# Rebalancing the first layer-norm tiles and moving two transposes in the head of an S5 + SwiGLU kernel

## The chip, the cores and the metric

One core of one Trainium2 chip. The metric is the device time of one execution in microseconds (us), smaller is better. The *span* that the profile shows is about 1.7 us shorter than that time, because it begins with the first profiled instruction and ends with the last. PE is TensorE, PEld its weight loads, DVE is VectorE, ACT is ScalarE, POOL is GpSimd, SP issues most DMAs. A time inside an execution is in us from the start of the span.

A run counts as slow when it is over 1.5% above the fastest of the same kernel.

## The reference, cut to what matters

The output is `x + A(xn) + B(xn)` with `xn = layernorm(x)` over 512 features, for 2048 rows. `A` is a linear state space (complex B matrix, scan over the rows, complex C matrix, skip term). `B` is a SwiGLU feed-forward of width 1376.

```python
xn = _layernorm(x)                                   # 2048 x 512
g, u = silu(xn @ w_gate), xn @ w_up                  # 512 x 1376 each
B = (g * u) @ w_down
Bu = einsum("bld,pd->blp", xn, B_bar)                # then h = Lam_bar*h + Bu[t], row by row
A = 2 * einsum("blp,dp->bld", hseq, Cmat).real + xn * Dskip
```

## The kernel before

The rows are worked in 4 chunks of 512 (4 tiles of 128 rows). Before PE can do anything useful, tile 0 must be loaded, normalised, transposed on PE and copied out of PSUM. To begin early, chunk 0's first seven gate column blocks are computed "in quarters": one 128-row tile after another, with the transposes of the next tile put between the matmuls. While waiting for tile 0, PE runs dummy matmuls.

The normalisation of the first tiles. Tile 0's left half is VectorE's, its right half ScalarE's; each tile has statistics (`b`, `s`), a reciprocal (`r`) and a normalisation in halves (`n`):

```python
def ln_half(a, h, order=()):
    cs = slice(h * 256, (h + 1) * 256)
    return g.add("dve", lambda e: e.tensor_scalar(out=xn_sb[:, a % NXN, cs], in0=x_sb[:, a, cs], scalar1=mv[:, a, 0:1], scalar2=rstd[:, a:a + 1],
                                                op0=ALU.subtract, op1=ALU.mult), ...)          # cut
# ... in ln_chunk0, VectorE's order:
for op, a, h in (("r", 0, 0), ("n", 0, 0), ("b", 1, 0), ("b", 1, 1), ("s", 1, 0), ("b", 2, 0),
                 ("r", 1, 0), ("n", 1, 0), ("n", 1, 1), ("b", 2, 1), ("s", 2, 0), ("b", 3, 0), ...):   # cut
    # ... with "r" of tile 0, ScalarE's part:
    g.add("act", lambda e: e.activation(out=xn_sb[:, 0, 256:512], in_=x_sb[:, 0, 256:512], func=AF.Identity, bias=nm0[:, 1:2], scale=rstd[:, 0:1]), ...)
```

The quarters. `place` says before which gate block (quarter, first contraction block, block number) the transposes of (tile, half) stand. All transposes of tiles 1 to 3 go through one PSUM bank, so each pair waits until the pair before has been copied out:

```python
place = {(0, 2, 4): (1, 0), (1, 0, 2): (1, 1), (1, 2, 2): (2, 0), (2, 0, 2): (2, 1), (2, 2, 1): (3, 0), (3, 0, 1): (3, 1)}
for q in range(4):
    for k0, k1 in (((0, 1), (1, 2), (2, 3), (3, 4)), ((0, 1), (1, 2), (2, 4)), ...)[q]:     # cut
        for n, (i, bk) in enumerate(tiles):                  # seven gate blocks
            if (q, k0, n) in place:
                xt_tile_fine(*place[(q, k0, n)])
            # ... k1 - k0 matmuls of 128 columns
```

After the quarters come one gate block of 512 columns, the up and gate blocks of chunk 0, and the state-space input `B_re`, `B_im`. Those two matrices come through DMA transposes. A DMA transpose is issued only when every DMA before it has landed, and every later DMA waits for it; so there is one long chain of DMAs: all first loads, B_re, B_im, the transpose of chunk 1, and so on.

```python
if xpose:
    after = after + tuple(dma_tasks)          # all DMAs before it
elif xp_state[0] is not None:
    after = after + (xp_state[0],)            # the last transpose
```

The order of instructions on VectorE, ScalarE and GpSimd is made by a list scheduler; that on PE and SP is the program's.

## Time and profile before

| | |
|---|---|
| time, median of 6 runs | 178.95 us (178.81 to 179.25) |
| PE busy | 173.5 us of the span of 177.2 us |
| first gate matmul of the quarters | 5.80 us |
| 512-column gate matmul after the quarters | 12.88 us |
| last addition on VectorE | starts 174.92 us |

The page of the kernel before: the span, the busy time and share of PE with its instructions, and two rows in which each digit is the busy share of a fortieth of the span, in tenths.

```profile
span 177.2 us, 2418 instructions
PE 173.5 (98%) x927; PEld 84.1 (47%) x935; DVE 162.7 (92%) x284; ACT 87.4 (49%) x116; POOL 11.1 (6%) x22
PE   8999999999999999999999999999999999999994
DMA  5892777662567500002000000001100000000032
```

PE is full from the first slice to the last. The DMA engines are loaded in the first 14 slices, and idle for most of the rest. So whatever a change does must show as an earlier or later start of PE's work, or as a gap in it.

PE's timeline in the head of the kernel before. The columns are start, duration of the merged group, engine, line, operation, tiles, shape, and count; matmuls overlap, so starts are the reliable part. Line L583 is the transposes, L478 the dummies, L804 the gate matmuls of the quarters, L760 the 512-column matmuls.

```profile
5.52 0.33 PE L583 MATMUL pb<-ident,xn_sb 128*128 128x128 bf16 x2
5.69 0.27 PE L478 MATMUL pb<-const-bfloat16-1.0 128*128 128x256 bf16 x1
5.80 1.17 PE L804 MATMUL pb<-xnT,wg 128*128 128x128 bf16 x18
6.80 0.28 PE L583 MATMUL pb<-ident,xn_sb 128*128 128x128 bf16 x2
...
8.63 0.28 PE L583 MATMUL pb<-ident,xn_sb 128*128 128x128 bf16 x2
8.74 0.83 PE L804 MATMUL pb<-xnT,wg 128*128 128x128 bf16 x12
9.53 0.27 PE L583 MATMUL pb<-ident,xn_sb 128*128 128x128 bf16 x2
...
12.88 0.38 PE L760 MATMUL pb<-xnT,wg 128*128 128x512 bf16 x1
```

ScalarE in the same stretch: its piece of tile 0 (L549), the first copy out of PSUM (an "eviction", L593), and the eviction of the pair of 8.63:

```profile
4.87 0.60 ACT L549 ACTIVATE xn_sb<-x_sb,nm,rstd 128x256 bf16<-128x256 bf16 x1
5.38 0.45 ACT L593 ACTIVATE xnT<-pb 128x128 bf16<-128x128 bf16 x2
8.95 0.45 ACT L593 ACTIVATE xnT<-pb 128x128 bf16<-128x128 bf16 x2 [0.62 <-PE pb L583]
```

Twelve matmuls at 55.8 ns are 0.67 us; from 8.74 to 9.53 it is 0.79. So 0.12 us is lost before the transposes at 9.53: they wait for ScalarE to copy the pair of 8.63 out of the shared bank, which takes it until 9.40.

The weight loads around the first use of B_im; in brackets, how long the loads stood idle, and what ended that:

```profile
23.89 0.74 PEld L881 LDWEIGHTS pb<-xnT,BT 128*128 128x128 bf16 x4
24.81 1.76 PEld L881 LDWEIGHTS pb<-xnT,BT 128*128 128x128 bf16 x9 [0.18 <-DMA BT<-in_A_B_im_dram]
```

```profile
174.92 0.29 DVE L983 TENSOR_TENSOR x_sb<-pb,x_sb 128x128 bf16<-128x128 f32 x1 [0.21 <-PE pb L978]
```

### The profile page before, as it was taken

To read this page: it belongs to the slowest core of one execution; us is meant where nothing else is said; L and a number is where in the kernel's file an instruction comes from. 1 tells how busy PE (TensorE), PEld (TensorE's weight loads), DVE (VectorE), ACT (ScalarE), POOL (GpSimd) and SP (SyncE) were. 2 spreads that over 40 slices of the span, in tenths; PEclk is the share of its full clock that TensorE was granted. 3 is DMA by queue.
4 is the path that set the end of the run, shared out by engine and by line. 5 is a ranking of instruction groups with operands and counts; after the bars stand their busy time and mean duration, and the time that the engine had idled before them with its cause. 6 is when DMAs were issued, how large, how long until landed. Compare 5 with 4: busy or idle time off the path is not lost.

```text
span 177.2 us, 2418 instructions
## 1 busy us (share of the span) xinstructions
PE 173.5 (98%) x927; PEld 84.1 (47%) x935; DVE 162.7 (92%) x284; ACT 87.4 (49%) x116; POOL 11.1 (6%) x22
## 2 busy tenths in 40 slices
PE   8999999999999999999999999999999999999994
PEld 2894444444444444444444444444444444444644
DVE  2965999899899999999999999999999999999943
ACT  4679989989979779220456554000365520000000
POOL 3040500050050000000000000000000000000000
DMA  5892777662567500002000000001100000000032
GB/s 167 273 372 81 122 129 112 171 143 70 142 130 269 113 7 0 0 4 89 31 0 0 0 0 4 0 0 59 59 0 4 0 0 0 0 0 32 31 110 68
DMA packets 22966, 12.37 MB, mean 70 GB/s; under 512 B 15180, under 2 KB 22956, under 8 KB 22956
## 3 DMA queue, kind: packets, MB, share of 16 engines
q1 hardware_dynamic: 22652, 11.77, 25.3%
q10 hardware_dynamic: 304, 0.46, 0.8%
q8 instruction: 7, 0.11, 0.3%
q14 instruction: 3, 0.02, 0.0%
HBM read 6.46 MB, written 2.10 MB: 48 GB/s over the span
## 4 chain that ended last, share of the span: by engine, by line
PE 60%; DMA 17%; DVE 15%; SPq 3%; issue 1%; POOL 1%; ACT 1%
PE pb L760 19%; PE pb L964 19%; PE pb L978 16%; DMA x_sb<-in_A_x_dram 7%; DVE rot L921 4%; PE pb L881 4%; SPq L405 3%; DVE st L483 3%; DMA xnT<-xn_sb 3%; DMA hss<-in_A_C_im_dram 3%; DVE rot L912 3%; DMA hss<-in_A_C_re_dram 2%; DMA dsk<-in_A_Dskip_dram 2%; PE pb L975 2%; DVE hT L832 2%
## 5 line engine op out<-in xcount | busy, mean ns | idle before, releaser
L921 DVE TENSOR_TENSOR_SCAN rot<-sm,car,rot 128x512 bf16<-128x512 f32 x32 | 38.9, 1266 | 0.0
L772 ACT ACTIVATE sg<-pb 128x1024 bf16<-128x1024 f32 x20 | 20.1, 1021 | 32.5 <-PE pb L760 31.8
L964 PE MATMUL pb<-wd,hT 128*128 128x512 bf16 (+2 forms) x176 | 34.5, 355 | 0.3 <-ACT uf L868 0.2
L978 PE MATMUL pb<-W,hss 128*128 128x512 bf16 (+2 forms) x140 | 29.7, 355 | 0.2
L760 PE MATMUL pb<-xnT,wu 128*128 128x512 bf16 x120 | 27.9, 379 | 0.0
L964 PEld LDWEIGHTS pb<-wd,hT 128*128 128x128 bf16 x180 | 16.8, 98 | 18.2 <-issue 0.4
L830 ACT ACTIVATE uf<-pb 128x1024 bf16<-128x1024 f32 x20 | 20.5, 1024 | 8.3 <-PE pb L760 8.0
L760 PE MATMUL pb<-xnT,wg 128*128 128x512 bf16 x92 | 21.8, 380 | 0.0
L881 PE MATMUL pb<-xnT,BT 128*128 128x512 bf16 x96 | 21.0, 380 | 0.0
L978 PEld LDWEIGHTS pb<-W,hss 128*128 128x128 bf16 x144 | 13.5, 97 | 14.4
L888 ACT ACTIVATE u_sb<-pb 128x1024 bf16<-128x1024 f32 x16 | 16.2, 1019 | 4.6 <-PE pb L881 4.6
L760 PEld LDWEIGHTS pb<-xnT,wu 128*128 128x128 bf16 x120 | 11.7, 98 | 14.2 <-issue 0.2
L881 PEld LDWEIGHTS pb<-xnT,BT 128*128 128x128 bf16 x96 | 9.4, 98 | 11.3 <-DMA BT<-in_A_B_im_dram 0.2
L983 DVE TENSOR_TENSOR x_sb<-pb,x_sb 128x512 bf16<-128x512 f32 (+2 forms) x18 | 11.1, 629 | 3.6 <-PE pb L978 3.0
L760 PEld LDWEIGHTS pb<-xnT,wg 128*128 128x128 bf16 x92 | 9.0, 98 | 10.6
L832 DVE TENSOR_TENSOR hT<-sg,uf 128x1024 bf16<-128x1024 bf16 x20 | 13.4, 681 | 0.3 <-ACT uf L830 0.3
L912 DVE TENSOR_TENSOR rot<-u_sb,cosT 128x2048 bf16<-128x2048 bf16 x8 | 9.7, 1218 | 0.1
L912 DVE TENSOR_TENSOR rot<-rot,sin 128x2048 bf16<-128x2048 bf16 x8 | 9.8, 1220 | 0.0
L912 DVE TENSOR_TENSOR rot<-u_sb,sin 128x2048 bf16<-128x2048 bf16 x8 | 9.7, 1217 | 0.0
L912 DVE TENSOR_TENSOR rot<-rot,cosT 128x2048 bf16<-128x2048 bf16 x8 | 9.7, 1215 | 0.0
L483 DVE BATCH_NORM_STATS2 st<-x_sb 128x6 f32<-128x512 bf16 x12 | 7.4, 680 | 2.4 <-DMA x_sb<-in_A_x_dram 2.4
L912 DVE TENSOR_TENSOR rot<-rot 128x2048 bf16<-128x2048 bf16 x8 | 9.6, 1217 | 0.0
(93 smaller groups left out, 180.9 us busy)
## 6 DMA issues: line engine op xcount, KB each, us to landing
out_dram<-x_sb SPq DMA_DIRECT2D x15, 128.0 KB, 1.7
x_sb<-in_A_x_dram SPq DMA_DIRECT2D x3, 512.0 KB, 4.7
wd<-in_B_w_down_dram SPq DMA_DIRECT2D x1, 1280.0 KB, 7.2
wu<-in_B_w_up_dram SPq DMA_DIRECT2D x1, 768.0 KB, 4.8
wu<-in_B_w_up_dram SPq DMA_DIRECT2D x1, 608.0 KB, 6.9
x_sb<-in_A_x_dram SPq DMA_DIRECT2D x4, 128.0 KB, 3.1
wg<-in_B_w_gate_dram SPq DMA_DIRECT2D x1, 480.0 KB, 5.8
wg<-in_B_w_gate_dram ACTq DMA_DIRECT2D x1, 448.0 KB, 3.8
```

The lines of the kernel that those rows point to most:

```text
L483: return g.add("dve", lambda e, a=a: e.bn_stats(out=st[:, a % 8, :], in_=x_sb[:, a, :]), reads=[("x", a)], writes=[("st", a % 8), ("st0", ...
L760: inst = e.matmul(pbank[0:fs, bk, :].rearrange("p (j t) -> p j t", j=4), lhsT=w[:, kt, i * 128:i * 128 + fs], rhs=xnT[c][:, :, kt, :], sta ...
L772: g.add("act", lambda e: e.activation(out=sg[rows, sl, 0:n, :].rearrange("p a t -> p (a t)"), in_=pair_f32(rows, bk, 512 * n), func=AF.Sil ...
L830: g.add("act", lambda e: e.activation(out=uf[rows, ul, 0:n, :].rearrange("p a t -> p (a t)"), in_=pair_f32(rows, bk, 512 * n), func=AF.Ide ...
L832: g.add("dve", lambda e: e.tensor_tensor(out=hT[rows, hb, i0:i0 + n, :], in0=sg[rows, sl, 0:n, :], in1=uf[rows, ul, 0:n, :], op=ALU.mult), ...
L881: inst = e.matmul(pbank[:, bk, :].rearrange("p (j t) -> p j t", j=4), lhsT=BT[:, ri, kt, pt * 128:(pt + 1) * 128], rhs=xnT[c][:, :, kt, :] ...
L888: g.add("act", lambda e: e.activation(out=u_sb[:, us].rearrange("p r t -> p (r t)"), in_=pair_f32(slice(0, 128), b0), func=AF.Identity), r ...
L912: tt = lambda out, a, b, op, r, w, nm: g.add("dve", lambda e: e.tensor_tensor(out=out, in0=a, in1=b, op=op), reads=r, writes=w, name="%s_% ...
L921: g.add("dve", lambda e, A0=A0, A1=A1, k=k, ri=ri, pt=pt: e.tensor_tensor_scan(out=A1[:, k, ri, :], data0=rr[:, pt:pt + 1].to_broadcast([1 ...
L964: inst = e.matmul(pbank[:, bk, 0:nc_], lhsT=hT[0:fs, hb, i, lt * 128:(lt + 1) * 128], rhs=wd[0:fs, i, c0:c0 + nc_], start=(i == 0), stop=F ...
L978: inst = e.matmul(pbank[:, bk, 0:nc_], lhsT=hss[:, hb, pt, ri, lt * 128:(lt + 1) * 128], rhs=W12[:, ri, pt, c0:c0 + nc_], start=False, sto ...
L983: g.add("dve", lambda e, bk=bk, a=a, c0=c0, nc_=nc_: e.tensor_tensor(out=x_sb[:, a, c0:c0 + nc_], in0=pbank[:, bk, 0:nc_], in1=x_sb[:, a, ...
```

## The change

The intent is a shorter head: give ScalarE less of tile 0, since PE waits for its half; take tile 1's statistics in one operation instead of two and a longer merge; and transpose the first halves of tiles 1 and 2 one gate block sooner, so that they are copied out before PE needs the bank and the data.

```diff
         def ln_half(a, h, order=()):
-            cs = slice(h * 256, (h + 1) * 256)
+            cs = slice(0, 384) if a == 0 else slice(h * 256, (h + 1) * 256)
 ...
-  in_=st0[:, a].rearrange("p h s -> p (h s)")[:, 0:6 if a == 0 else 12]),
-  reads=[("st0", a, 0), ("st0", a, 1)], writes=[("mv", a)], ...
+  in_=st0[:, a].rearrange("p h s -> p (h s)")[:, 0:6 if a < 2 else 12]),
+  reads=[("st0", a, h) for h in range(1 if a < 2 else 2)], writes=[("mv", a)], ...
 ...
-            for op, a, h in (("r", 0, 0), ("n", 0, 0), ("b", 1, 0), ("b", 1, 1), ("s", 1, 0), ("b", 2, 0),
+            for op, a, h in (("r", 0, 0), ("n", 0, 0), ("B", 1, 0), ("s", 1, 0), ("b", 2, 0),
 ...
-  e.activation(out=xn_sb[:, 0, 256:512], in_=x_sb[:, 0, 256:512], ...
+  e.activation(out=xn_sb[:, 0, 384:512], in_=x_sb[:, 0, 384:512], ...
 ...
-            place = {(0, 2, 4): (1, 0), (1, 0, 2): (1, 1), (1, 2, 2): (2, 0), ...
+            place = {(0, 2, 3): (1, 0), (1, 0, 2): (1, 1), (1, 2, 1): (2, 0), ...
```

Cut: the second transposes of a tile now wait for both of its parts, and "B" calls the 512-column statistics. After the head, the order of instructions is the same on every engine.

More of the change, by code (lines that the diff above doesn't have):

```diff
@@ L522, in ln_stat0 @@
         def ln_stat0(a, order):
-            t = g.add("dve", lambda e: e.bn_aggr(out=mv[:, a, :], in_=st0[:, a].rearrange("p h s -> p (h s)")[:, 0:6 if a == 0 else 12]),
-                      reads=[("st0", a, 0), ("st0", a, 1)], writes=[("mv", a)], name="bnag%d" % a, est=160, order=order)
+            t = g.add("dve", lambda e: e.bn_aggr(out=mv[:, a, :], in_=st0[:, a].rearrange("p h s -> p (h s)")[:, 0:6 if a < 2 else 12]),
+                      reads=[("st0", a, h) for h in range(1 if a < 2 else 2)], writes=[("mv", a)], name="bnag%d" % a, est=160, order=order)
             hold["sd%d" % a] = g.add("act", lambda e: e.activation(out=sd0[:, a:a + 1], in_=mv[:, a, 1:2], func=AF.Sqrt, bias=epst[:, 0:1]),
@@ L548, in ln_chunk0 @@
                         hold["nmr0"] = g.tasks[-1]
-                        g.add("act", lambda e: e.activation(out=xn_sb[:, 0, 256:512], in_=x_sb[:, 0, 256:512], func=AF.Identity, bias=nm0[:, 1:2], scale=rstd[:, 0:1]),
-                              reads=[("x", 0), ("rstd", 0), ("nm0", 1)], writes=[("xh", 0, 1)], name="xn0_1", est=430)
+                        g.add("act", lambda e: e.activation(out=xn_sb[:, 0, 384:512], in_=x_sb[:, 0, 384:512], func=AF.Identity, bias=nm0[:, 1:2], scale=rstd[:, 0:1]),
+                              reads=[("x", 0), ("rstd", 0), ("nm0", 1)], writes=[("xh", 0, 1)], name="xn0_1", est=400)
                         hold["xa01"] = g.tasks[-1]
@@ L555, in ln_chunk0 @@
                     last = bn_half(a, h, (last,))
+                elif op == "B":
+                    last = bn_full(a, (last,))
                 elif op == "p":
@@ L585, in tr2 @@
                 return inst
-            g.add("pe", tr2, reads=[("xh", a, h), ("ident",)], writes=BK(slot), name="xT%d_%d" % (a, h), est=2 * 64, ninst=2)
+            g.add("pe", tr2, reads=[("xh", a, k) for k in range(h + 1)] + [("ident",)], writes=BK(slot), name="xT%d_%d" % (a, h), est=2 * 64, ninst=2)
             dst, src = xnT[0][:, a % 4, 2 * h:2 * h + 2, :], ptr[:, slot, 0:256].rearrange("p (k t) -> p k t", k=2)
@@ L794, in ffn_gate_quarters @@
             pe_warm(1, 256, tiles[-2][1])
-            place = {(0, 2, 4): (1, 0), (1, 0, 2): (1, 1), (1, 2, 2): (2, 0), (2, 0, 2): (2, 1), (2, 2, 1): (3, 0), (3, 0, 1): (3, 1)}
+            place = {(0, 2, 3): (1, 0), (1, 0, 2): (1, 1), (1, 2, 1): (2, 0), (2, 0, 2): (2, 1), (2, 2, 1): (3, 0), (3, 0, 1): (3, 1)}
             for q in range(4):
```

## The prediction

> **What bounds the kernel now.** TensorE: the page has PE busy 98% of the 177.2 us span, and the table by stretches has it busy for all of 5.80 to 12.88 us (chunk 0's gate matmuls, in quarters) and 12.88 to 24.10. The change touches only the head, before 12.9 us. What counts is when the first gate matmul starts (5.80), stalls inside the quarters, and whether an earlier head reaches the end.
>
> **The edits, costed.**
> - VectorE takes 384 columns of tile 0, not 256: the timeline has 345 ns for 256 and 406 ns for 512, so +30 ns. The first transposes (4.97 us) and ScalarE's first eviction (5.38) start up to 0.03 later.
> - ScalarE takes 128 columns, not 256 (measured 600 ns). The Trainium skill, "ScalarE: Activation LUTs", What ACT_TABLE_LOAD costs, has 0.833 ns per element and 93 ns per pointer operand over 186 ns: 585 ns for 256 with two pointers, in agreement. So -107 ns, an estimate. The waits view has PE waiting 0.3 us for this result; the second transposes should move from 5.52 to about 5.42.
> - The first gate matmul also needs the first eviction, which gets no earlier: gain 0.03 to 0.1 us (start about 5.73).
> - Tile 1 statistics: two half ops take 0.75 us, one full op 0.695, the aggregate of 6 values 183 ns instead of 208: -0.08, less the +0.03 above. Tile 1's normalisation comes 0.05 earlier, enough for its earlier transposes, with at most 0.05 of wait.
> - Transposes one gate tile sooner: two 56 ns matmuls move behind them, no work changes. At 55.8 ns a matmul and 0.11 us a pair of transposes, the quarters have some 0.15 us of stall in 7.08, 0.12 of it before 9.53 us, where PE waits for tile 2's eviction. That should go.
>
> Head gain: about 0.15 us (0.05 to 0.25); quarters end near 12.73.
>
> **How much reaches the end: almost nothing.** At 24.81 us PE waits for the DMA transpose of B_im. The waits view says 0.18 us; at the pitch of 0.216 us the load was due at 24.75, so the loss is 0.06. The chain of waits has only DMAs there: x tiles 4 to 7 land at 15.99, B_re runs from 16.03 to 20.48, B_im from 20.50 to 24.8. These wait for no engine, the DMA share is 0.98 from 5.8 to 12.9 us, and the edit moves no DMA. PE arrives earlier and waits longer by as much. A second such place is 67.71 us, where PE waits 0.16 us for a ScalarE eviction behind DMA and VectorE work. The order of instructions after the head is unchanged on every engine.
>
> **Predicted: 178.8 us** (before 178.9), 8 in 10 between 178.4 and 179.2. Faster by over 2%: 0.005; within 2%: 0.99; slower: 0.005.
>
> **What would show it.** Right: second transposes near 5.42, first gate matmul 5.70 to 5.80, transposes of tile 1 near 6.68 and of tile 2 near 8.45 without a wait, the gap before 9.5 gone, quarters ending near 12.73; then PE's weight load waiting about 0.3 us for B_im, still at 24.8, and PE's times as before from there. Wrong: B_im landing earlier with the head, or PE's times after 24.8 shifted by the head gain; or a later head (transposes waiting for normalisation, gate matmul after 5.85), which would reach the end nearly in full, since only 0.06 us of slack is there.
>
> **What could make it wrong.** DMA landings that scatter by more than the head gain, and the scatter of runs (178.81 to 179.25), larger than the edit's effect.

## More of the kernel before

PE where the last transpose is first used (the second line), and VectorE's last addition:

```profile
63.82 1.03 PE L843 MATMUL pb<-scrC,wg 128*128 128x512 bf16 x4
64.68 1.03 PE L843 MATMUL pb<-xnT,wg 128*128 128x512 bf16 x4
```

## The result, and the profile after

| | before | after |
|---|---|---|
| median of 6 runs, us | 178.95 (178.81 to 179.25) | 178.98 (178.77 to 179.23) |
| ratio of fast runs | | 1.0001 (0.9988 to 1.0014) |
| first gate matmul, us | 5.80 | 5.52 |
| tile 1's transposes, us | 6.80 | 6.75 |
| 512-column gate matmul, us | 12.88 | 12.72 |
| last addition starts, us | 174.92 | 175.10 |

Ratios are the mean time of one kernel's fast runs over that of the other's of the same rounds, so they are not quite the ratios of the medians. The time is the same; the interval is about 0.2 us to either side. The head ends 0.16 us earlier, and in this profile the end comes 0.18 us later.

The page of the changed kernel:

```profile
span 177.4 us, 2425 instructions
PE 173.9 (98%) x935; PEld 83.8 (47%) x935; DVE 162.5 (92%) x283; ACT 86.9 (49%) x116; POOL 11.1 (6%) x22
```

The counts of PE differ only because 8 matmul records are missing in the trace before. Line numbers behind the edits are 2 higher. PE's timeline in the head of the changed kernel, and ScalarE's piece of tile 0 and first eviction:

```profile
5.29 0.29 PE L585 MATMUL pb<-ident,xn_sb 128*128 128x128 bf16 x2
5.41 0.27 PE L478 MATMUL pb<-const-bfloat16-1.0 128*128 128x256 bf16 x1
5.52 1.39 PE L806 MATMUL pb<-xnT,wg 128*128 128x128 bf16 x17
6.75 0.27 PE L585 MATMUL pb<-ident,xn_sb 128*128 128x128 bf16 x2
...
8.48 0.28 PE L585 MATMUL pb<-ident,xn_sb 128*128 128x128 bf16 x2
8.59 0.94 PE L806 MATMUL pb<-xnT,wg 128*128 128x128 bf16 x14
9.37 0.28 PE L585 MATMUL pb<-ident,xn_sb 128*128 128x128 bf16 x2
...
12.72 0.59 PE L762 MATMUL pb<-xnT,wg 128*128 128x512 bf16 x2
```

```profile
4.74 0.49 ACT L549 ACTIVATE xn_sb<-x_sb,nm,rstd 128x128 bf16<-128x128 bf16 x1
5.17 0.45 ACT L595 ACTIVATE xnT<-pb 128x128 bf16<-128x128 bf16 x2
```

Two things are to be seen. From 8.59 to 9.37 there are now 14 matmuls in 0.78 us, at 55.8 ns each: the stall is gone. But 17 matmuls from 5.52 to 6.75 take 1.23 us where 0.95 would do. The starts of the single matmuls have a gap of 0.28 us before 6.58 us: the third contraction block's gate weights landed at 6.45 us here, at 6.07 in the trace before. So the early start (5.52) was lost again at 6.58, which is also when the same matmul ran before (5.80 + 14 x 0.0558 = 6.58). Only the stalls taken out of the quarters remain.

The weight loads at B_im, PE at the last transpose, and the last addition, after:

```profile
23.73 0.74 PEld L883 LDWEIGHTS pb<-xnT,BT 128*128 128x128 bf16 x4
24.75 1.67 PEld L883 LDWEIGHTS pb<-xnT,BT 128*128 128x128 bf16 x9 [0.27 <-DMA BT<-in_A_B_im_dram]
```

```profile
63.66 1.03 PE L845 MATMUL pb<-scrC,wg 128*128 128x512 bf16 x4
64.85 1.04 PE L845 MATMUL pb<-xnT,wg 128*128 128x512 bf16 x4 [0.17 <-DMA xnT<-xn_sb]
```

```profile
175.10 0.29 DVE L985 TENSOR_TENSOR x_sb<-pb,x_sb 128x128 bf16<-128x128 f32 x1 [0.21 <-PE pb L980]
```

The loads waited 0.27 us for B_im, but the matmuls show no gap over 0.03 us at 24.8: loads run ahead of matmuls. PE was still 0.16 us ahead of the trace before at 37.76 (37.92 before) and at 63.66 (63.82 before). Then four matmuls that were due at 64.52 (4 x 0.2157 after 63.66) came at 64.85: the last transpose had landed only at 64.81 us (62.74 in the trace before). That gap of 0.33 us turned a lead of 0.16 into a lag of 0.18. Its cause lies earlier in the DMA chain: the transpose is issued when the loads of `w_down` have landed, which was at 60.48 us here and at 58.43 before. The change touches no DMA, so I took it for scatter and tested that.

### The profile page after: what moved, and what is told of

It is laid out like the page before. It is cut to its first block, busy times and chain, and to the rows that moved or that the text cites. A ratio compares the mean times of both kernels' runs of the same rounds, so it can differ in the third digit from the quotient of the medians.

```text
span 177.4 us, 2425 instructions
## 1 busy us (share of the span) xinstructions
PE 173.9 (98%) x935; PEld 83.8 (47%) x935; DVE 162.5 (92%) x283; ACT 86.9 (49%) x116; POOL 11.1 (6%) x22
## 3 DMA queue, kind: packets, MB, share of 16 engines
HBM read 6.46 MB, written 2.10 MB: 48 GB/s over the span
## 4 chain that ended last, share of the span: by engine, by line
PE 62%; DMA 19%; DVE 7%; ACT 4%; SPq 3%; POOL 1%; issue 1%; ACTq 0%
PE pb L966 20%; PE pb L762 19%; PE pb L980 16%; DMA x_sb<-in_A_x_dram 7%; DMA xnT<-xn_sb 5%; PE pb L883 4%; SPq L405 3%; DVE st L483 3%; DMA hss<-in_A_C_im_dram 3%; DMA hss<-in_A_C_re_dram 2%; DMA dsk<-in_A_Dskip_dram 2%; PE pb L977 2%; ACT xn_sb L507 2%; DVE hT L834 1%; PE pb L855 1%
## 5 line engine op out<-in xcount | busy, mean ns | idle before, releaser
L966 PE MATMUL pb<-wd,hT 128*128 128x512 bf16 (+2 forms) x180 | 35.2, 355 | 0.0
L980 PE MATMUL pb<-W,hss 128*128 128x512 bf16 (+2 forms) x144 | 30.3, 355 | 0.0
```

Source lines behind the costliest of these rows:

```text
L966: inst = e.matmul(pbank[:, bk, 0:nc_], lhsT=hT[0:fs, hb, i, lt * 128:(lt + 1) * 128], rhs=wd[0:fs, i, c0:c0 + nc_], start=(i == 0), stop=F ...
L980: inst = e.matmul(pbank[:, bk, 0:nc_], lhsT=hss[:, hb, pt, ri, lt * 128:(lt + 1) * 128], rhs=W12[:, ri, pt, c0:c0 + nc_], start=False, sto ...
```

## The experiments

My theories going in: (A) the prediction's, that the DMA chain swallows any head gain at 24.8 us; (B) that the gain reaches the end unless the run happens to be late somewhere; and, for the head, which of the three parts does the work. The kernels that change PE's amount or order of work keep the order of all other engines on purpose: the estimates that the scheduler sees were left as they were, and the orders were compared.

### Before, again

No edit.

> The kernel before, unchanged, profiled a second time, to see what scatters by itself. If head and DMA times scatter from run to run: the first gate matmul between 5.5 and 5.8 us (depending on when TensorE's clock steps up), x tiles 4 to 7 landing anywhere from 15.9 to 16.4 us, B_im used first at 24.7 to 25.0, and the span 177.1 to 177.5. If instead these differences between the two traces are caused by the change: first gate matmul again at 5.80 within 0.03, landing at 15.99, and no wait for the last transpose (xnT of chunk 3) near 64.8.

Time 179.3 us against 178.82 for another run of the same kernel. The first gate matmul came at 5.99 us, outside the 5.5 to 5.8 that I expected, since its weights landed at 5.86 us (5.01 in the first trace), the 512-column gate matmul at 13.17 and the last addition at 175.21. So the same kernel moves by 0.29 us from one trace to the next, in the head and, undiminished, at the end. The x tiles 4 to 7 landed at 16.32 (15.97 in the first trace), the last transpose at 63.47 (62.74). The scatter is larger than the change.

### One part at a time

Only the transposes' place:

```diff
-            place = {(0, 2, 4): (1, 0), (1, 0, 2): (1, 1), (1, 2, 2): (2, 0), ...
+            place = {(0, 2, 3): (1, 0), (1, 0, 2): (1, 1), (1, 2, 1): (2, 0), ...
```

> Only the earlier place of the first-half transposes of tiles 1 and 2. My theory: the stall of 0.12 us before the transposes near 9.5 us goes, and the stretch from the first gate matmul to the 512-column gate matmul takes 6.95 to 7.0 us instead of 7.08, less whatever the gate weights' landing adds; a wait of at most 0.1 us may appear before tile 1's transposes, whose normalisation is not earlier here. Rival (the gain in the quarters comes from the statistics or the split): the stretch stays at 7.05 to 7.1.

The whole stretch took 7.42 us, against the 6.95 to 7.0 that I expected, but not by stalls. PE's timeline of this kernel:

```profile
5.52 0.42 PE L478 MATMUL pb<-const-bfloat16-1.0 128*128 128x256 bf16 x1
5.73 1.61 PE L804 MATMUL pb<-xnT,wg 128*128 128x128 bf16 x17
7.17 0.28 PE L583 MATMUL pb<-ident,xn_sb 128*128 128x128 bf16 x2
```

The starts of its first gate matmuls are 0.107 us apart up to 6.69 us, and 0.056 after. This is TensorE's clock at half rate: in this run it stepped up at about 6.7 us, in the changed kernel's profile before 4.85. The dummy of 256 columns just before the first gate matmul (0.42 us here, 0.27 after the step) tells at a glance which it is. From tile 1's transposes on, it was 5.98 us with no gap over 0.03 us, so the part does what was expected.

Only the 384/128 split of tile 0:

```diff
-            cs = slice(h * 256, (h + 1) * 256)
+            cs = slice(0, 384) if a == 0 else slice(h * 256, (h + 1) * 256)
-  in_=x_sb[:, 0, 256:512], func=AF.Identity, bias=nm0[:, 1:2] ...
+  in_=x_sb[:, 0, 384:512], func=AF.Identity, bias=nm0[:, 1:2] ...
```

> Only the 384/128 split of tile 0. My theory: the ScalarE piece takes about 0.49 us instead of 0.60, the second transposes come 0.07 to 0.12 us sooner after the reciprocal, the first gate matmul 0.03 to 0.1 us sooner after it; the stall of 0.12 us before 9.5 us stays. Rival (the whole 0.28 us of the first gate matmul came from the split): 0.25 us or more from the same reciprocal to the first gate matmul.

ScalarE's piece took 493 ns (600 before), and the second transposes came 1.13 us after the reciprocal's start (5.33 after 4.20), against 1.24 to 1.26 in the two traces of the kernel before: 0.11 to 0.13 us sooner. In all 14 traces it was 1.07 to 1.14 us in the eight with the split and 1.18 to 1.25 in the six without. The first gate matmul came at 5.73 us, 1.54 us after the reciprocal's start (1.52 in the first trace before), so the 0.03 to 0.1 us that I expected there did not show in this run; and, with the clock slow up to about 6.7 us, tile 1's transposes only at 7.22. Two stalls of 0.12 us stayed in the quarters. So the split gives its 0.1 us at the second transposes, and not the whole 0.28 of the first gate matmul, whose parts are listed further below.

Only tile 1's statistics in one operation:

```diff
-  ("n", 0, 0), ("b", 1, 0), ("b", 1, 1), ("s", 1, 0), ("b", 2, 0),
+  ("n", 0, 0), ("B", 1, 0), ("s", 1, 0), ("b", 2, 0),
-  [:, 0:6 if a == 0 else 12]
+  [:, 0:6 if a < 2 else 12]
```

> Only the one-op statistics of tile 1. My theory: tile 1's aggregate starts about 0.05 us sooner after tile 0's normalisation, its normalisation 0.05 to 0.08 sooner, and nothing on PE moves, since PE reached tile 1's transposes without waiting before; stretch from the first gate matmul to the 512-column one 7.05 to 7.1 us as before. Rival (tile 1's normalisation was holding PE): the transposes of tile 1 come 0.05 us or more sooner after the first gate matmul.

The aggregate began 0.98 us after tile 0's normalisation (5.37 after 4.39), where before it was 1.04 and 1.05: 0.06 sooner. Tile 1's normalisation, which I expected sooner too, was not: 1.84 us after tile 0's, against 1.81 in the first trace before. The quarters kept their stall (0.12 us before 9.55), and from tile 1's transposes to the 512-column matmul it was 6.08 us, as before. Nothing on PE moved. The stretch from the first gate matmul was 7.28 us and not the 7.05 to 7.1 expected: 0.20 of it is a gap at 6.34 us, with the third block's gate weights landing at 6.46. The time, 180.13 us, came from elsewhere. PE's timeline near 58 us:

```profile
59.78 3.63 PE L883 MATMUL pb<-scrC,BT 128*128 128x512 bf16 x16 [0.96 <-ACT sg L774]
```

PE stood still for 1.12 us between 58.44 and 59.78, waiting for a PSUM bank that ScalarE empties. ScalarE had itself idled 1.8 us for VectorE before normalising chunk 3. Smaller gaps at this place turn up in other runs below, with both orders of the head.

### Taking work out of the head

Half of the contraction is left out of four up blocks, 8 matmuls of 512 columns or 1.73 us of PE. Its output is wrong, which doesn't matter for the time.

```diff
-                ffn_mm(c, i0 + k, "u", bk + k)
+                ffn_mm(c, i0 + k, "u", bk + k, 2 if c == 0 and ip < 2 else KT)
```

> The changed kernel with 8 matmuls of 512 columns (4 x 2, the up projection of chunk 0, half the contraction left out) taken from PE between 13.6 and 24 us; wrong on purpose, all other engines' order kept. It makes the head gain 8 x 0.216 = 1.73 us instead of 0.15. My theory (the DMA chain fixes when PE may go on at 24.8 us): PE waits about 1.9 to 2.0 us for B_im instead of 0.27, later PE times unmoved, span and time unchanged within 0.15 us. Rival (the wait at 24.8 us is an accident of the profile, and a head gain reaches the end): time 1.5 to 1.8 us lower, near 177.3.

Ratio 0.9993 (0.9965 to 1.0021); median 178.98 us, before 179.16 on the same chip. The rival's 1.5 us is excluded. The weight loads, PE near 59 us and the last addition:

```profile
25.16 1.41 PEld L883 LDWEIGHTS pb<-xnT,BT 128*128 128x128 bf16 x8 [1.87 <-DMA BT<-in_A_B_im_dram]
```

```profile
59.26 3.63 PE L883 MATMUL pb<-scrC,BT 128*128 128x512 bf16 x16 [0.25 <-ACT sg L774]
```

```profile
175.55 0.29 DVE L985 TENSOR_TENSOR x_sb<-pb,x_sb 128x128 bf16<-128x128 f32 x1 [0.21 <-PE pb L980]
```

Here the matmuls did stop, for 1.55 us, at B_im, which landed at 25.11; another 0.42 us went at 59.26. Together they ate the 1.73 us, and 0.24 more. A large head gain is thus swallowed at 24.8 us, as theory A has it.

### Adding work to the head

Six dummy matmuls, 1.29 us, just behind the quarters, for both kernels:

```diff
+            pe_warm(6, 512, xt_pair[0])
+            g.tasks[-1].est = 0.0
             ffn_mm(0, NQ, "g", xt_pair[0])
```

> The changed kernel with 6 dummy matmuls of 512 columns (1.29 us) put on PE just after the quarters, order otherwise kept. My theory: about 0.2 us of it is swallowed by the wait for B_im, and up to 0.2 us more by the wait for the last transpose near 64.8 us, the rest reaches the end: time 0.85 to 1.15 us higher than before, near 179.95. Rival (the DMA chain alone sets the time up to 67 us): time within 0.3 us of before. Second rival (there is no slack at all): 1.3 us higher.

> The kernel before with the same 6 dummy matmuls (1.29 us) after the quarters as head_plus6 has. PE then comes 1.2 us later to B_im and to the last transpose, so neither should hold it, and a head difference should pass to the end undiminished. Revised theory: from tile 1's transposes to the 512-column gate matmul 7.38 to 7.47 us (head_plus6 has 7.35), the last addition 162.04 us after that matmul, no PE gap after it but the switch to 64 columns; time 179.9 to 180.5, its difference from head_plus6 (180.13) too small for the times. Rival (the gap goes to some later wait even so): a PE gap after 25 us, and the last addition more than 162.1 us after the gate matmul.

Changed kernel with the dummies: median 180.13 us, ratio to before 1.0058 (1.0033 to 1.0082), which is 0.6 to 1.5 us. Kernel before with the dummies: 180.48 us, 1.0081 (1.0065 to 1.0096). The first rival of head_plus6 (less than 0.3 us) is excluded; 0.85 to 1.15 and 1.29 are not told apart by the times. The traces do it. The last additions, first of the changed kernel, then of the kernel before:

```profile
176.06 0.29 DVE L987 TENSOR_TENSOR x_sb<-pb,x_sb 128x128 bf16<-128x128 f32 x1 [0.22 <-PE pb L982]
```

```profile
175.97 0.29 DVE L985 TENSOR_TENSOR x_sb<-pb,x_sb 128x128 bf16<-128x128 f32 x1 [0.21 <-PE pb L980]
```

The 512-column gate matmul ran at 14.03 and at 13.93 us. To the last addition it was 162.03 and 162.04 us, without a gap that other runs don't have. With PE late, nothing is given back anywhere: a microsecond in the head is a microsecond at the end. The kernel before was even 0.10 us ahead of the changed one here, because its head began earlier: the first gate matmul ran at 5.54 us against 5.73, after a reciprocal that was 0.09 us sooner and with the clock stepping up at about 3.7 us instead of 5.6. (In neither did PE wait for the third block's weights.) That one run of each cannot be turned into a difference of the kernels.

### Giving B_im and the last transpose more room

A helper moves one group of PE's matmuls behind another after scheduling. `after_slack` puts B_re of the second block ahead of B_im of the first; `two_gates` and `late_gates` also ask for the last transpose later, in two ways.

```diff
+        pe_after("mm_b0_0_1", "mm_b0_1_0")           # all three
+        pe_after("mm_ul0", "mm_g1_%d" % FL)          # two_gates
+        pe_after("mm_g3_%d" % FL, "mm_ul2")          # late_gates
```

> The changed kernel with two groups of 4 PE matmuls exchanged (B_re of the second block before B_im of the first), so that B_im is needed 0.86 us later. My theory: the wait of 0.2 to 0.3 us at 24.8 goes; PE runs 0.2 to 0.3 us earlier until the last transpose near 64.8 us, where it waits by so much longer if that lands late, as in the changed kernel's profile, and passes where it lands early, as in the profile before; time 0 to 0.25 us lower. Rival (B_im's wait doesn't matter): the same times, PE at 64 us as before.

> As after_slack, and the left-over up matmuls of chunks 0 and 1 moved ahead of the gate matmuls of chunks 2 and 3, so that the last transpose is needed 1.7 us later as well. My theory: neither wait is left, PE runs unbroken from the quarters to the end, the head gain arrives: time 0.2 to 0.45 us lower than before, near 178.6. Rival (something else, ScalarE's or VectorE's chain at 67 us, fixes the rest): within 0.1 us of before.

> The changed kernel with B_im and the last transpose both needed 0.86 us later (B_re of the second block before B_im of the first; the left-over gate matmuls of chunk 3 behind the left-over up matmuls, without a further switch between 64 and 128 columns). Theory: no PE gap at 24.8 or near 64.5, end 162.04 us after the 512-column gate matmul; time 0.1 to 0.3 us below before's (ratio 0.998 to 0.9995), which 5 rounds may or may not tell from 1. Rival (the late chain through VectorE and ScalarE near 56 us holds PE): a gap near 58 us and no gain.

Ratios to before: after_slack 0.9986 (0.9959 to 1.0013), two_gates 0.9994 (0.9969 to 1.0018), late_gates 0.9998 (0.9966 to 1.003). None is told from 1. The gaps at 24.8 and 64.5 us were absent in all three traces. two_gates paid 0.2 us for two more switches between matmuls that use 128 and those that use 64 columns of PE's array (`128*128` and `128*64` in the profile; 0.09 to 0.10 us each). late_gates met the third place instead, which my theory for it had not counted:

```profile
58.95 3.63 PE L883 MATMUL pb<-scrC,BT 128*128 128x512 bf16 x16 [0.28 <-ACT sg L774]
```

That is a gap of 0.45 us, behind the chain through VectorE and ScalarE, and its last addition started at 175.25. In this trace its rival was right. No version was found that beats both kernels by an amount the times can show.

### Changed kernel and place alone, with more times

No edit to the changed kernel; the place alone as above.

> The changed kernel, unchanged, for more times and a second trace. Revised theory: the transposes one tile sooner always take 0.12 to 0.2 us of stall out of the quarters, so from tile 1's transposes to the 512-column gate matmul 5.97 to 6.03 us (before 6.08 and 6.17); the wait for B_im takes no more than 0.05 us of it, and from the 512-column gate matmul to the last addition it is 162.04 us plus the later stalls of the run. So the head gain reaches the end wherever nothing else is late, on average 0.05 to 0.2 us, below what the times can show (ratio 0.998 to 1.0015). Rival (the prediction: swallowed at 24.8 us in every run): the first B_im matmul waits for its landing, the stretch from the 512-column gate matmul to the last addition is longer than 162.04 by the head gain, 162.1 to 162.25, from a gap near 24.8.

> Only the earlier transposes, for times. Revised theory: this is the one part whose gain is the same in every run; from tile 1's transposes to the 512-column gate matmul 5.97 to 6.03 us, time as the changed kernel's within 0.15 us. Rival (the three parts are needed together): 6.08 or more, because tile 1's normalisation isn't earlier here.

after_again: median 179.15 us, before 179.16, ratio 0.9995 (0.9961 to 1.0029). place_repeat: 179.05 us, 0.9995 (0.9958 to 1.0032). The changed kernel's second trace, at B_im, at the last transpose and at the end:

```profile
24.77 1.64 PEld L883 LDWEIGHTS pb<-xnT,BT 128*128 128x128 bf16 x9 [0.30 <-DMA BT<-in_A_B_im_dram]
```

```profile
64.52 1.03 PE L845 MATMUL pb<-xnT,wg 128*128 128x512 bf16 x4
```

```profile
174.76 0.29 DVE L985 TENSOR_TENSOR x_sb<-pb,x_sb 128x128 bf16<-128x128 f32 x1 [0.22 <-PE pb L980]
```

The 512-column gate matmul is again at 12.72, the loads wait 0.30 us for B_im, and yet no matmul is late, there or at 64.52. The last addition is at 174.76, 0.16 us before that of the first trace of the kernel before (174.92). In this run the whole head gain reached the end. In place_repeat the head ended at 12.71, just as early, but x tiles 4 to 7 landed at 16.95 us, B_im at 25.88, and PE stopped:

```profile
25.92 0.55 PEld L881 LDWEIGHTS pb<-xnT,BT 128*128 128x128 bf16 x4 [1.45 <-DMA BT<-in_A_B_im_dram]
```

```profile
176.27 0.29 DVE L983 TENSOR_TENSOR x_sb<-pb,x_sb 128x128 bf16<-128x128 f32 x1 [0.22 <-PE pb L978]
```

A gap of 1.12 us there and one of 0.37 us at 59.98 gave it the latest last addition of all the traces, later even than with 1.29 us of dummies.

### All traces in one table

"Quarters" is the time from tile 1's transposes to the 512-column gate matmul (in the rows with dummies less 1.29 us). "Rest" is from that matmul to the last addition. Gaps are read from the starts of PE's matmuls, above the pitch of 0.2157 us; a gap that comes from a missing record, and the two switches to and from matmuls with 64 columns of the array that every trace has, are not listed.

| trace | place of transposes | quarters | 512-column matmul | last addition | rest | gaps in the rest |
|---|---|---|---|---|---|---|
| before | old | 6.08 | 12.88 | 174.92 | 162.04 | none |
| before_again | old | 6.17 | 13.17 | 175.21 | 162.04 | none |
| split_only | old | 6.15 | 13.37 | 175.42 | 162.05 | none |
| stats_only | old | 6.08 | 12.90 | 176.07 | 163.17 | 1.12 at 58 |
| before_plus6 | old | 6.10 | 13.93 | 175.97 | 162.04 | none |
| after | new | 5.97 | 12.72 | 175.10 | 162.38 | 0.33 at 64.5 |
| after_again | new | 6.00 | 12.72 | 174.76 | 162.04 | none |
| place_only | new | 5.98 | 13.15 | 175.19 | 162.04 | none |
| place_repeat | new | 5.99 | 12.71 | 176.27 | 163.56 | 1.12 at 25, 0.37 at 59 |
| head_plus6 | new | 6.06 | 14.03 | 176.06 | 162.03 | none |
| head_minus8 | new | 6.00 | 13.25 | 175.55 | 162.30 (1.73 less work) | 1.55 at 24, 0.42 at 59 |
| after_slack | new | 5.98 | 12.93 | 174.97 | 162.04 | none |
| two_gates | new | 5.98 | 12.70 | 174.96 | 162.26 | two more switches |
| late_gates | new | 5.98 | 12.75 | 175.25 | 162.50 | 0.45 at 58 |

The last addition comes 162.04 us after the 512-column gate matmul, plus the gaps. The five old quarters average 6.12 us, the nine new 5.99; one matmul of 0.056 us more falls into the new stretch, so the earlier place takes about 0.18 us of stall out. No new stretch is as long as any old one.

## Why the prediction was right, and which steps of it were not

- **Time, 178.8 in 178.4 to 179.2, within 2%.** Measured 178.98, ratio 1.0001. Right. But the time alone does not bear out the mechanism: had all of the 0.16 us reached the end, 178.8 would have been in the range as well.
- **Costs of the operations.** The ScalarE piece was estimated at 600 - 107 = 493 ns and measured 493 (the formula of the Trainium skill, "ScalarE: Activation LUTs", What ACT_TABLE_LOAD costs, gives an estimate of 479 for 128 columns with two pointer operands). VectorE's 384 columns took 378 ns (345 + 30 expected). Second transposes sooner by about 0.1 us: 0.11 to 0.13 alone. Statistics: nothing on PE moved. The stall at 9.5 us: gone. Quarters ending near 12.73: 12.72, and 12.72 again. Right, with some luck: with the same place of the transposes, the quarters of other runs without dummies ended at 12.70 to 13.25.
- **"The first gate matmul also needs the first eviction, which gets no earlier: gain 0.03 to 0.1 us (start about 5.73)": wrong in the profile after, 5.52.** In the profile before, that eviction had ended at 5.65 us and did not hold the matmul of 5.80: PE ran the second transposes, a dummy and the gate matmul one behind the other, so the gate matmul moves with the second transposes. And the eviction did get earlier (5.38 to 5.17), because the program puts it on ScalarE behind the piece of tile 0 that became shorter. The 0.28 us are 0.06 from the reciprocal (4.28 to 4.21, as tile 0 landed at 2.92 and not 2.98), 0.06 from ScalarE's start on its piece (0.53 us after the reciprocal and not 0.59; both occur with either kernel), 0.11 from the shorter piece, and 0.05 from the clock: matmuls ran at half rate until about 5.6 us in before's trace, until some time before 4.85 in after's. And the gain there was worth nothing, which the prediction did not see: in the profile after, the third block's weights landed at 6.45 us and held PE until 6.58. That the head gain came out right is owed to the stalls in the quarters.
- **"PE arrives earlier and waits longer by as much", with the loss of 0.06 us at 24.81: wrong for a gain of this size.** I read the wait of the weight load as a loss of PE. The matmul that needs B_im was due 56 x 0.2157 = 12.08 us after 12.88, at 24.96; B_im had landed at 24.77, and a matmul that does wait starts some 0.05 us after the landing (25.11 to 25.16, 25.88 to 25.92). So the kernel before had about 0.15 us to spare there, just the size of the head gain. The changed kernel uses that up and loses only where B_im lands later than about 24.75 us. The mechanism is real (1.55 us swallowed in head_minus8, 1.12 in place_repeat), but its threshold was 0.2 us off.
- **"A second such place is 67.71 us": wrong.** What looks like a wait there is the switch from 64 to 128 columns plus a missing matmul record; it is in every trace. The places that do stop PE late in some runs are 58 us and 64.5 us.
- **"almost nothing reaches the end": not shown.** In one of the two traces of the changed kernel all of the 0.16 us reached the end, in the other it was lost at 64.5 us. The times cannot decide: 0.16 us is 0.0009 of the time, and the intervals are 0.0013 and 0.0034 wide to either side. What the runs do show is that the effect on the time is at most about a quarter of a us either way.

Why the large change in the head moves the time so little is thus: it is worth about 0.18 us, one part in a thousand. Gate weights landing from 6.04 to 6.87 us, the clock stepping up from about 3.6 to about 6.7 us, and three late places with gaps of up to 1.12 us move single runs by more. Open are why the landings scatter by up to 1 us, and the change's mean effect below 0.1%. That the late transpose at 64.8 us is scatter and not an effect of the change is supported by after_again (landed at 63.26, no gap), though two traces are few. The 14 traces together leave a doubt: from the landing of x tiles 4 to 7 to that of the last transpose it took 45.3 to 47.2 us in the five with the old place and 45.4 to 48.9 in the nine with the new one, six of them longer than any old one. No run was made to tell whether the change lengthens that chain, so this is open too.

## What to carry to other kernels

Where PE is full from the head to the end, first find the landings that PE nearly waits for, and compare each with the time when the *matmul*, not its weight load, is due; a head gain counts only up to the smallest such margin, and a head loss counted in full here (1.29 us, in both traces with dummies). Take several traces before trusting a difference of a few tenths of a microsecond between two: here one kernel's own head varied by 0.3 us. To learn whether a stretch is on the critical path, take out or add ten times the expected gain there, as with the 8 removed and 6 added matmuls, which one look at the times can tell.

## What the Trainium skill lacked or had wrong

- "TensorE: Matmul & The Clock Gate", What you observe: the step to the full clock is put at around 4 us of sustained matmuls, give or take 0.5 us from run to run. In 14 traces with the same dummy matmuls from 0.83 us on, it came at about 3.6 us (three traces: the 512-column dummies go from 0.427 to 0.220 us apart) to about 6.7 us (two traces), which is 2.7 to 5.9 us after the first; from about 4.2 us on, PE had waits of up to 0.7 us between its matmuls. The pace agrees with the page (0.107 and 0.056 us for 128 columns). The granted clock in the stretches of these profiles said 1.00 throughout, so it did not show the slow phase; only the starts of the matmuls did.
- "Perfetto Trace Analysis", Tensor Engine Instruction, says of loads to a background buffer that this "has not been investigated thoroughly", and no page that I read says that a weight load's wait in a profile need not be a loss of PE. In after_again a weight load waited 0.30 us for its data and the matmuls had no gap over 0.03 us.
- "DMA: Bandwidth & Descriptors", Latency and other measured facts, has 261 GB/s for a DMA transpose whose middle dimension is not contiguous, and some 350 to 400 where it is. B_im, 0.52 MB, took 3.9 us from issue to landing in the changed kernel's trace, 134 GB/s with the fixed part included; the page gives no figure for a single transpose of this size.
- No page that I read tells how much landings scatter between executions of one kernel: here the x tiles 4 to 7 landed between 15.75 and 16.95 us in the 14 traces.
- No page that I read gives the time that a switch between matmuls with 128 and with 64 columns of the array costs (it would belong to "TensorEngine Tiling (Array Packing)"): 0.09 to 0.10 us of PE here.
